# Layer 2's gate and value products by one level of Strassen, and the exponentials divided in place on GpSimd

## The chip, the core and the metric

The kernel runs on one core of one Trainium2 chip. Its engines work side by side, each through its own queue in order: TensorE (PE in the rows; PEld is its weight load), VectorE (DVE), ScalarE (ACT), GpSimd (POOL), and SyncE (SP), which issues the DMAs. The metric is the device time of one execution in microseconds.

## The reference

```python
# attention: batch 2, 12 heads, 448 positions, head dimension 64
scores = (1 / np.sqrt(64)) * np.matmul(q, k.transpose(0, 1, 3, 2))
scores = np.where(mask, -1e9, scores)              # causal
attn = np.exp(scores - np.max(scores, axis=-1, keepdims=True))
attn = attn / (np.sum(attn, axis=-1, keepdims=True) + 1e-09)
x = np.matmul(attn, v)                             # then 896 tokens x 768
# layer 1: d_ff 2048
h = x @ w_in
g = (a[0] + a[1] * h + a[2] * h**2 + a[3] * h**3) / (1 + abs(b[0]) * abs(h) + abs(b[1]) * h**2 + 1e-6)
x = g @ w_out
# layer 2: d_ff 1536
gate = 1.0 / (1.0 + np.exp(-(x @ w_gate)))
val = x @ w_val
return (gate * val) @ w_out
```

The weights come as float64 and are turned into float32 on the chip.

## The kernel before

Every product of the two layers is made of three matmuls: both operands are split into a high part (fp32r) and a low part (what is left), and high x high, high x low and low x high are summed in PSUM. So a weight costs, after its DMA on SP (`raw`, 768 KB), two ScalarE passes and one VectorE pass that make float32 (`val`), a copy to the high part and a subtraction on GpSimd for the low part (`weight`, L145 to L176). An activation costs a copy (ScalarE) and a subtraction (GpSimd).

**Attention** runs over 12 pairs of heads, each in three groups of query tiles, (0, 1), (2), (3), of 112 queries each; a tile t has (t+1) x 112 keys. For a group: `scores` on TensorE (L442), `maximum` on VectorE with the mask (L450), `exponentials` on ScalarE with the row sum (L464), `turn`, which transposes the exponentials on TensorE (L482), `copied` out of PSUM (L490, L492), and at the end of the pair `values`, the product with v (L519). The exponentials are not divided. In their place `inverses` (L470, L471) makes the reciprocals of the sums, once a pair; `factors` (L501) spreads them over the 64 rows of a head by small matmuls against the identity; `factors_out` (L511) copies them out on ScalarE; `result` (L528) multiplies the values by them on VectorE; `result_hi` (L535) and `result_lo` (L540, GpSimd but for the last pair of a batch) split the result into `xh` and `xl`.

**Layer 1** goes in 4 chunks of 512 features and two parts of the tokens (0 to 447 and 448 to 895 in chunk 0, 0 to 383 and 384 to 895 afterwards): `in1_tile` gives h, `rational` g (six VectorE operations a tile, L275 to L285), `out1_tile` sums into `y1` and, in the last chunk, splits y1 into xh and xl again (L331, L334).

**Layer 2** goes in 6 chunks of 256 features and the two parts of the tokens: `gate_tile` and `val_tile` (both through `up`, L252 to L258), 6 steps along d_model for each block of 128 features, then the sigmoid, the product and its split (L355 to L361); `out2_tile` (L365) sums 14 output tiles of 128 x 384 into `y2` (L389), one chunk at a time, and the last chunk writes them out (L392). The first gate tile is woven between the last output tiles of layer 1 (`woven("1110111", ...)`).

**The order.** All work is listed as jobs with an engine, an estimated cost, what they wait for and a rank. `in_turn` (L36) plays them through: on each engine the ready job with the lowest rank goes next. The order found is fixed as the order of each queue. TensorE's order of the two layers' products is a chain (`unit`); attention's steps run two groups ahead (`LA = 2`), with two PSUM tiles for scores and transposes in turn, and the products of layer 1's chunk 0 fill gaps among them. Weights come in `portion`s through two raw and two val buffers in turn.

## Time and profile before

| | |
|---|---|
| median of three timed runs | 603.45 us |
| the three runs | 603.12, 603.45, 603.87 us |
| span of the profiled execution, first to last instruction | 601.4 us |
| TensorE busy | 593.5 us (99%) |
| VectorE, ScalarE, GpSimd busy | 358.0, 357.2, 254.4 us |
| attention with the first products of layer 1 | 0 to about 124 us |
| layer 1 | to about 344 us |
| layer 2 | to 598 us, the last write to 601.4 us |

A busy share is an average; which engine ends a stretch is read from the chain of waits and from the stretches one by one. Matmuls are pipelined, so a matmul's own duration in a row is longer than its share of TensorE's time; the distance between two starts is that share.

### The profile page before, as it was taken

What the parts mean: (1) busy time and instruction counts of PE and PEld (TensorE: products, weight loads), DVE (VectorE), ACT (ScalarE), POOL (GpSimd) and SP (SyncE); (2) the same over time, 40 slices, a digit from 0 to 9 for tenths busy, and PEclk for the clock granted to TensorE, in tenths of its full rate; (3) what the DMA queues carried; (4) which work ended last, traced back from release to release, by engine and by line L of the source; (5) the groups of instructions that cost most, each with busy time, mean ns of one, the idle gap of its engine ahead of it and who ended that gap; (6) DMA issues with size and microseconds to landing.
All of it is one profiled execution on the core that took longest, in us unless ns stands there. A gap on an engine that the chain in (4) does not pass through costs nothing.

```text
span 601.4 us, 8821 instructions
## 1 busy us (share of the span) xinstructions
PE 593.5 (99%) x3352; PEld 511.6 (85%) x3352; DVE 358.0 (60%) x677; ACT 357.2 (59%) x686; POOL 254.4 (42%) x193
## 2 busy tenths in 40 slices
PE   7999999999999999999999999999999999999997
PEld 5566666689988998898898989989989989989987
DVE  5877899938968986789685243246336335312314
ACT  6888888858897793859396448766344444111010
POOL 0634321357529656534746465545145144211010
PEclk9999999999999999999999999999999999999999
DMA  7645340045413351323421054645324123000004
GB/s 242 207 173 158 118 166 16 6 157 166 146 53 110 108 195 53 113 88 123 152 59 51 2 158 158 210 157 161 102 105 159 54 105 106 0 1 1 0 14 170
DMA packets 25641, 65.05 MB, mean 108 GB/s; under 512 B 1984, under 2 KB 3776, under 8 KB 25600
## 3 DMA queue, kind: packets, MB, share of 16 engines
q1 hardware_dynamic: 25600, 64.50, 32.7%
q8 instruction: 26, 0.43, 0.3%
q14 instruction: 15, 0.12, 0.1%
HBM read 61.74 MB, written 2.75 MB: 107 GB/s over the span
## 4 chain that ended last, share of the span: by engine, by line
PE 97%; DVE 2%; issue 0%; ACT 0%; DVEq 0%
PE h L256 7%; PE o L314 6%; PE h L258 6%; PE h L257 6%; PE o L315 6%; PE o L316 6%; PE z L381 5%; PE z L379 5%; PE z L380 5%; PE gu L257 5%; PE gu L258 5%; PE gu L256 5%; PE vu L257 5%; PE vu L256 5%; PE vu L258 5%; PE s L442 4%
## 5 line engine op out<-in xcount | busy, mean ns | idle before, releaser
L361 POOL TENSOR_TENSOR gl<-pr_u,gh 128x384 fp32r<-128x384 f32 (+1 forms) x24 | 27.7, 1153 | 111.5 <-ACT gh L359 111.5
L289 POOL TENSOR_TENSOR gl_h<-t_h,gh_h 128x384 fp32r<-128x384 f32 (+2 forms) x32 | 39.2, 1226 | 84.0 <-ACT gh_h L287 83.9
L256 PE MATMUL h<-xh,wh_in 128*128 128x384 f32 (+2 forms) x192 | 71.3, 371 | 0.0
L314 PE MATMUL o<-gh_h,oh_out 128*128 128x384 f32 (+2 forms) x192 | 70.3, 366 | 0.0
L315 PE MATMUL o<-gl_h,oh_out 128*128 128x384 f32 (+2 forms) x192 | 69.9, 364 | 0.0
L316 PE MATMUL o<-gh_h,ol_out 128*128 128x384 f32 (+2 forms) x192 | 69.9, 364 | 0.0
L258 PE MATMUL h<-xh,wl_in 128*128 128x384 f32 (+2 forms) x192 | 69.7, 363 | 0.0
L257 PE MATMUL h<-xl,wh_in 128*128 128x384 f32 (+2 forms) x192 | 69.7, 363 | 0.0
L176 POOL TENSOR_TENSOR ol_out<-val_out,oh_out 128x768 fp32r<-128x768 f32 x28 | 55.1, 1971 | 26.7 <-ACT oh_out L174 25.4
L389 DVE TENSOR_TENSOR y<-y,z 128x384 f32<-128x384 f32 x70 | 38.3, 552 | 32.2 <-PE z L381 32.1
L357 DVE TENSOR_TENSOR pr_u<-sg_u,vu 128x384 f32<-128x384 f32 (+1 forms) x24 | 14.8, 617 | 70.8 <-PE vu L258 68.4
L381 PE MATMUL z<-oh_out,gl 128*128 128x384 f32 x168 | 56.2, 335 | 0.0
L379 PE MATMUL z<-oh_out,gh 128*128 128x384 f32 x168 | 56.2, 335 | 0.0
L380 PE MATMUL z<-ol_out,gh 128*128 128x384 f32 x168 | 56.2, 334 | 0.0
L164 DVE SCALAR_TENSOR_TENSOR val_out<-raw_out 128x768 uint32<-128x768 uint32 x28 | 35.7, 1277 | 31.3 <-ACT raw_out L161 23.4
L464 ACT ACTIVATE e<-e,sc 112x112 f32<-112x112 f32 (+3 forms) x96 | 49.7, 522 | 6.5 <-DVE sc L450 6.3
L258 PE MATMUL gu<-xh,wl_gate 128*128 128x384 f32 (+1 forms) x144 | 52.2, 363 | 0.0
L257 PE MATMUL gu<-xl,wh_gate 128*128 128x384 f32 (+1 forms) x144 | 52.2, 363 | 0.0
L257 PE MATMUL vu<-xl,wh_val 128*128 128x384 f32 (+1 forms) x144 | 52.1, 362 | 0.0
L256 PE MATMUL gu<-xh,wh_gate 128*128 128x384 f32 (+1 forms) x144 | 52.1, 362 | 0.0
L256 PE MATMUL vu<-xh,wh_val 128*128 128x384 f32 (+1 forms) x144 | 52.1, 362 | 0.0
L258 PE MATMUL vu<-xh,wl_val 128*128 128x384 f32 (+1 forms) x144 | 52.1, 362 | 0.0
(89 smaller groups left out, 1425.5 us busy)
## 6 DMA issues: line engine op xcount, KB each, us to landing
raw_out<-in_moe_w_out_dram SPq DMA_DIRECT2D x28, 768.0 KB, 4.3
raw_in<-in_moe_w_in_dram SPq DMA_DIRECT2D x16, 768.0 KB, 4.5
raw_gate<-in_moe_w_gate_dram SPq DMA_DIRECT2D x12, 768.0 KB, 4.3
raw_val<-in_moe_w_val_dram SPq DMA_DIRECT2D x12, 768.0 KB, 4.3
qk<-in_qk_dram SPq DMA_DIRECT2D x12, 448.0 KB, 5.7
v<-in_v_dram SPq DMA_DIRECT2D x12, 224.0 KB, 3.8
out_dram<-y SPq DMA_DIRECT2D x14, 192.0 KB, 1.8
a_sb<-in_moe_a_dram SPq DMA_DIRECT2D x1, 2.0 KB, 7.1
```

The costliest lines, as they stand in the source:

```text
L176: nc.gpsimd.tensor_tensor(lo, vf, hi, op=ALU.subtract)
L256: nc.tensor.matmul(ps, hi[:, c, fs], xh[:, c, bs], start=(c == 0), stop=False)
L257: nc.tensor.matmul(ps, hi[:, c, fs], xl[:, c, bs], start=False, stop=False)
L258: nc.tensor.matmul(ps, lo[:, c, fs], xh[:, c, bs], start=False, stop=(c == KC - 1))
L289: nc.gpsimd.tensor_tensor(gl, t, gh, op=ALU.subtract)
L314: nc.tensor.matmul(ps, hi[:, es], gh, start=(i == 0), stop=False)
L315: nc.tensor.matmul(ps, hi[:, es], gl, start=False, stop=False)
L316: nc.tensor.matmul(ps, lo[:, es], gh, start=False, stop=(i == NF - 1))
L379: nc.tensor.matmul(ps, gh[:, ms], hi[:, ns], start=(i == 0), stop=False)
L380: nc.tensor.matmul(ps, gh[:, ms], lo[:, ns], start=False, stop=False)
L381: nc.tensor.matmul(ps, gl[:, ms], hi[:, ns], start=False, stop=(i == NF2 - 1))
L464: nc.scalar.activation(e, e, AF.Exp, bias=d["sc"][:, t, j : j + 1], scale=-1.0, accum_out=d["sum"][:, t, j : j + 1])
```

## The change

**Strassen in layer 2.** For one unit (a block of 128 features, of gate and value together) the two weights are the rows of a 2 x 2 matrix of blocks, gate and value by the lower and upper half of d_model; the activations are the columns, lower and upper half of d_model by the first and second 448 tokens. Winograd's form makes the four results from seven block products in place of eight. Sums of weights (`weight_sums`, four a unit) and of activations (`act_sum`, once) are made in float32 first and then split into high and low. Each block product is 3 steps of 3 matmuls of 448 columns. Four PSUM banks A to D hold the products of a unit; `combine` adds them up, some in PSUM itself. Weights and activations lie in two large rooms cut up by hand, ten slots for weights. There are 12 units; the output products go over groups of two units, but the last two groups have one unit each. The order at the seam is: all of layer 1's output tiles, then units 0 (in an order of its own), 1 and 2, then output groups and units in turn.

**Division in place.** `inverses` runs for each group, `normalised` multiplies the exponentials by the reciprocals on GpSimd before they are transposed, and `factors`, `factors_out` and `result` go. The values in PSUM are split straight away, `result_lo` on VectorE always. The values get a second PSUM tile.

The planner's ranks and costs are set anew, and it takes in a cost for a change of TensorE's tiling mode. The diff, cut to its core:

```diff
+    PRODUCTS = {
+        "p1": ("a11", "b11", "A", True),
+        "p6": ("s2", "t2", "B", True),
+        "p7": ("s3", "t3", "C", True),
+        "p5": ("s1", "t1", "D", True),
+        "p2": ("a12", "b21", "A", False),
+        "p4": ("a22", "t4", "C", False),
+        "p3": ("s4", "b22", "D", False),
+    }
...
+    def weight_sums(u, k):
+        a = {n: halves[u, n] for n in ("a11", "a12", "a21", "a22", "s1", "s2", "s3", "s4")}
+        if k == 0:
+            nc.vector.tensor_tensor(a["s1"], a["a21"], a["a22"], op=ALU.add)
+            nc.vector.tensor_tensor(a["s2"], a["s1"], a["a11"], op=ALU.subtract)
+        else:
+            nc.vector.tensor_tensor(a["s3"], a["a11"], a["a21"], op=ALU.subtract)
+            nc.vector.tensor_tensor(a["s4"], a["a12"], a["s2"], op=ALU.subtract)
...
+    def weight_hi(u, name):
+        nc.scalar.copy(slot(u, name)[0], halves[u, PRODUCTS[name][0]])
+    def weight_lo(u, name):
+        hi, lo = slot(u, name)
+        nc.gpsimd.tensor_tensor(lo, halves[u, PRODUCTS[name][0]], hi, op=ALU.subtract)
...
+    def act_lo(name, c):
+        eng = nc.vector if name in BY_VECTOR else nc.gpsimd
+        eng.tensor_tensor(act[name][1][:, c], act_from(name, c), act[name][0][:, c], op=ALU.subtract)
+    def product(u, name, c):
...
+        nc.tensor.matmul(ps, hi[:, c], bh[:, c], start=begins, stop=False, skip_group_check=True)
+        nc.tensor.matmul(ps, hi[:, c], bl[:, c], start=False, stop=False, skip_group_check=True)
+        nc.tensor.matmul(ps, lo[:, c], bh[:, c], start=False, stop=ends, skip_group_check=True)
+    def combine(u, what):
...
+        if what == "p1":
+            nc.scalar.copy(x, ps["A"])
+        elif what == "u2":
+            nc.vector.tensor_tensor(x, x, ps["B"], op=ALU.add)
+        elif what == "u3":
+            nc.vector.tensor_tensor(y, x, ps["C"], op=ALU.add)
+        elif what == "c22":
+            nc.vector.tensor_tensor(y, y, ps["D"], op=ALU.add)
+        elif what == "sg1":
+            nc.scalar.activation(z, ps["A"], AF.Sigmoid)
+        elif what == "c21":
+            nc.vector.tensor_tensor(ps["C"], x, ps["C"], op=ALU.add)
+        elif what == "pr1":
+            nc.vector.tensor_tensor(z, z, ps["C"], op=ALU.mult)
+        elif what == "c12":
+            nc.vector.tensor_tensor(ps["D"], x, ps["D"], op=ALU.add)
+        elif what == "sg2":
+            nc.scalar.activation(ps["D"], ps["D"], AF.Sigmoid)
+        elif what == "pr2":
+            nc.vector.tensor_tensor(y, y, ps["D"], op=ALU.mult)
...
-    def inverses(n):
-        rs = T[n]["sum"]
+    def inverses(n, k):
+        rs = T[n]["sum"][:, GROUPS[k][0] : GROUPS[k][-1] + 1]
         nc.vector.tensor_scalar_add(rs, rs, 1e-9)
         nc.vector.reciprocal(rs, rs)
+    def normalised(n, t, j):
+        e = T[n]["e", t, j]
+        nc.gpsimd.tensor_scalar(e, e, T[n]["sum"][:, t, j : j + 1], 1.0, op0=ALU.mult, op1=ALU.mult)
...
     def result_hi(n):
-        nc.scalar.copy(xh[x_part(n)], T[n]["xn"])
+        nc.scalar.copy(xh[x_part(n)], T[n]["x"])
     def result_lo(n):
-        eng = nc.vector if pairs[n][1] == NP - 1 else nc.gpsimd
-        eng.tensor_tensor(xl[x_part(n)], T[n]["xn"], xh[x_part(n)], op=ALU.subtract)
+        nc.vector.tensor_tensor(xl[x_part(n)], T[n]["x"], xh[x_part(n)], op=ALU.subtract)
...
-            [("exp", n, t, j) for t in GROUPS[k] for j in both] + freed_by("s"),
-            rank + R_TURN,
+            [("norm", n, t, j) for t in GROUPS[k] for j in both] + freed_by("s"),
+            rank + R["turn"],
...
+    GROUPS2 = [(u, u + 1) for u in range(0, NU - 2, 2)] + [(NU - 2,), (NU - 1,)]
...
-    woven("1110111", stage_in2(0, 0), stage_out(*ins[-1]))
+    _run(stage_out(*ins[-1]))
+    sums_of_x()
+    unit_of_weights(0, ("p1", "p5", "p2", "p7", "p6", "p4", "p3"))
+    unit_of_weights(1, PRODUCTS)
+    unit_of_weights(2, PRODUCTS)
```

## Rows read from the trace of the kernel before

**Rows 1.** The page: TensorE's busy time, granted clock and DMA rate by slice.

```profile
PE 593.5 (99%) x3352; PEld 511.6 (85%) x3352; DVE 358.0 (60%) x677; ACT 357.2 (59%) x686; POOL 254.4 (42%) x193
...
PEclk9999999999999999999999999999999999999999
...
GB/s 242 207 173 158 118 166 16 6 157 166 146 53 110 108 195 53 113 88 123 152 59 51 2 158 158 210 157 161 102 105 159 54 105 106 0 1 1 0 14 170
```

**Rows 2.** The page, the chain that ended last: shares of the span by engine.

```profile
PE 97%; DVE 2%; issue 0%; ACT 0%; DVEq 0%
```

**Rows 3.** Stretches: length, busy time of PE, PEld, DVE, ACT, POOL; clock; DMA.

```profile
0.00:124.00 124.00, 119.63 (x928) 76.04 (x929) 98.72 (x302) 100.89 (x274) 39.96 (x39) 1.00 0.42 138
80.00:100.00 20.00, 20.00 (x148) 13.67 (x146) 17.79 (x50) 16.32 (x45) 4.93 (x4) 1.00 0.17 51
120.00:140.00 20.00, 20.00 (x104) 17.17 (x103) 8.55 (x9) 11.55 (x18) 11.80 (x8) 1.00 0.49 157
345.00:601.40 256.40, 252.89 (x1324) 235.50 (x1322) 97.04 (x123) 98.71 (x146) 87.05 (x57) 1.00 0.30 97
```

**Rows 4.** TensorE in order of time: start, duration, line, first matmuls of a stage.

```profile
134.06 0.37 PE L256 MATMUL h<-xh,wh_in 128*128 128x448 f32 x1
...
148.94 0.34 PE L256 MATMUL h<-xh,wh_in 128*128 128x384 f32 x1
...
161.43 0.36 PE L314 MATMUL o<-gh_h,oh_out 128*128 128x448 f32 x1
...
523.35 0.39 PE L256 MATMUL gu<-xh,wh_gate 128*128 128x512 f32 x1
...
539.71 0.33 PE L379 MATMUL z<-oh_out,gh 128*128 128x384 f32 x1
```

**Rows 5.** The chain in order of time: start, time on the chain, what.

```profile
5.60 0.28 DVE e L450
...
21.30 0.92 PE r L501 x16
...
121.45 2.04 PE x L519 x16
```

**Rows 6.** VectorE's groups, 0 to 124 us: count, busy us, mean ns, idle before.

```profile
L528 DVE TENSOR_TENSOR xn<-xn,x 128x448 f32<-128x448 f32 x12 | 7.4, 614 | 2.2 <-PE x L519 1.9 <-ACT xn L511 0.3
...
L470 DVE TENSOR_SCALAR sum<-sum 112x8 f32<-112x8 f32 x12 | 3.6, 300 | 0.0
...
L284 DVE SCALAR_TENSOR_TENSOR d_h<-z_h,one,d_h 128x448 f32<-128x448 f32 x4 | 2.7, 685 | 0.1
...
L471 DVE RECIPROCAL sum<-sum 112x8 f32<-112x8 f32 x12 | 2.4, 203 | 0.4
```

**Rows 7.** VectorE and GpSimd in order of time around 64.5 us.

```profile
64.45 1.83 POOL L176 TENSOR_TENSOR ol_out<-val_out,oh_out 128x768 fp32r<-128x768 f32 x1
...
64.54 1.77 DVE L470 TENSOR_SCALAR sum<-sum 112x8 f32<-112x8 f32 x1
```

**Rows 8.** GpSimd's groups over the span, shapes apart.

```profile
L176 POOL TENSOR_TENSOR wl_val<-val_val,wh_val 128x768 fp32r<-128x768 f32 x12 | 23.5, 1958 | 15.6 <-ACT wh_val L174 13.7 <-PE z L381 1.8
...
L361 POOL TENSOR_TENSOR gl<-pr_u,gh 128x512 fp32r<-128x512 f32 x12 | 15.5, 1291 | 53.9 <-ACT gh L359 53.9
...
L172 POOL TENSOR_SCALAR oh_out<-val_out 128x768 fp32r<-128x768 f32 x16 | 13.4, 836 | 16.2 <-DVE val_out L164 15.1 <-PE o L315 1.0
...
L361 POOL TENSOR_TENSOR gl<-pr_u,gh 128x384 fp32r<-128x384 f32 x12 | 12.2, 1015 | 57.6 <-ACT gh L359 57.6
...
L334 POOL TENSOR_TENSOR xl<-y,xh 128x448 fp32r<-128x448 f32 x6 | 7.6, 1272 | 1.6 <-ACT xh L331 1.6
```

**Rows 9.** One first group, in order of time: its last row sum, its transposes.

```profile
48.40 0.20 ACT L464 ACTIVATION_READ_ACCUMULATOR e<-e,sc 112x1 f32 x1
...
51.12 0.79 PE L482 MATMUL p<-ident,e 112*112 112x112 f32 x6
```

**Rows 10.** VectorE's timeline: four output sums in a row.

```profile
320.63 1.94 DVE L326 TENSOR_TENSOR y<-y,o 128x384 f32<-128x384 f32 x4
```

More of the change, by code (lines that the diff above doesn't have):

```diff
@@ L365, in out2_tile @@
-    def out2_tile(c, m, n):
-        half = m // 4
+    PRODUCTS = {
[7 more added lines that the diff above has]
+    }
+    first, second = slice(0, S), slice(S, NT)
+    lows, highs = slice(0, KH), slice(KH, KC)
+    act = {"b11": (xh[:, lows, first], xl[:, lows, first]), "b21": (xh[:, highs, first], xl[:, highs, first])}
@@ new lines, in combine @@
+    def combine(u, what):
+        ps = {b: unit_ps.get((u, b)) for b in "ABCD"}
+        if what in ("p1", "u3", "sg1"):
+            n = {"p1": "x", "u3": "y", "sg1": "z"}[what]
+            unit_sb[u, n] = tmp.tile([P, 512], F32, tag="t1" if n == "y" else "t0", name=f"{n}_{u}")[:, :S]
+        x, y, z = (unit_sb.get((u, n)) for n in "xyz")
+        gh, gl = store["g"][u % NG2]
+        if what == "p1":
[18 more added lines that the diff above has]
+            nc.vector.tensor_tensor(y, y, ps["D"], op=ALU.mult)
+        else:
+            t, ns = (z, first) if what[-1] == "1" else (y, second)
+            if what[:2] == "gh":
+                nc.scalar.copy(gh[:, ns], t)
+            else:
+                nc.gpsimd.tensor_tensor(gl[:, ns], t, gh[:, ns], op=ALU.subtract)
@@ L368, in out2_tile @@
+    def out2_tile(group, m_, n):
+        us = GROUPS2[group]
+        half = m_ // 4
         if half not in y2:
@@ L692, in tile_causal_attention__moe_rational__moe_glu, with weights_out2 @@
+    def weights_out2(u):
+        key = ("out2", u, 0)
+        free = [("out", NCH - 1, 1, KC - 1, "mm", NF - 1)]
+        if u >= 4:
+            group = next(k for k, us in enumerate(GROUPS2) if u - 4 in us)
+            free = [("out2", group, ready[B] - 1, 1, "mm", len(GROUPS2[group]) - 1)]
+        group = next(k for k, us in enumerate(GROUPS2) if u in us)
+        portion((*key, 0), rows(wt, key, w_out2, u), free, ("out2", group, 0, 0, "mm", GROUPS2[group].index(u)))
     tiles = {}
     unit = None
-    n_tiles = [0, 0]
+    n_tiles = [0, 0, 0]
@@ L712, in place @@
         n_tiles[after] += 1
-        ring = "b" if after and n_tiles[1] % 6 > 1 else "a"
-        deps = freed_by(ring, 4 if ring == "b" else 2) + ["late"] * after
-        freed[ring].append([(*key, "after", read)])
+        if key[:3] == ("out", NCH - 1, 1) or key[0] == "out2":
+            n_tiles[2] += 1
+            r = "ad"[n_tiles[2] // 2 % 2]
+        else:
+            r = "b" if after and n_tiles[1] % 6 > 1 else "a"
+        deps = freed_by(r, 4 if r == "b" else 2) + ["late"] * after
+        freed[r].append([(*key, "after", read)])
+        ring[key] = r
         return deps
@@ L764, in stage_out @@
                 matmuls(key, i, deps + [("out", c, i, 0, 5), ("in", c, b, i, "after", 5)], UNIT[width(c, b)], out1_tile)
-            follow(key, scaled(stages, c, b, 0.15 * (c > 0) * b), at["end"] + R_SUM)
+            follow(key, scaled(stages, c, b, 0.15 * (c > 0) * b), at["end"] + R["sum"])
             yield
-    def stage_in2(c, b):
-        for i in range(NF2):
-            kg, kv = ("gate", c, b, i), ("val", c, b, i)
-            for key, make in ((kg, gate_tile), (kv, val_tile)):
-                deps = place(kv, 0 if key == kg else 1)
-                for u in range(KC):
-                    w = [(key[0], c, 0, u // 3, 5), ("out", NCH - 1, b, u, "after", 2)]
-                    matmuls(key, u, deps + w, UNIT[width(1, b)], make)
-            followed(kv, scaled(GLU, 1, b), ("out2", c, ready[b], 0, "mm", i), [("in", NCH - 1, 1, NF - 1, "after", 2)])
-            yield
@@ new lines, in stage_out2 @@
+    def stage_out2(group):
+        stages = [("ACT", 0.48) if group == 0 else ("DVE", 0.55)]
+        if group == len(GROUPS2) - 1:
+            stages.append(("SP", 0.1))
+        sums = [("out", NCH - 1, k, KC - 1, "after", 2) for k in range(B)] + [("tl", "t4", KH - 1)]
+        for b in range(B):
+            for m in range(ready[b], ready[b + 1]):
+                for n in range(2):
+                    key = ("out2", group, m, n)
+                    deps = place(key, 0) + (sums if group == 0 else [])
+                    for i, u in enumerate(GROUPS2[group]):
+                        gs = [("e", u, f"gl{k + 1}") for k in range(b + 1)]
+                        matmuls(key, i, deps + [("out2", u, 0, 0, 5), *gs], UNIT2, out2_tile)
+                    follow(key, stages, at["end"] + R["sum"])
+                    yield
```

405 lines of the change are left out of this document (258 added, 147 removed).

## The prediction, made before the change was built

> **What bounds the kernel now.** I read the page's first two parts before anything else: TensorE is busy 99% of the span, and its granted clock is full in every slice, which is the 2.4 GHz level [rows 1]. A busy share of matmuls can flatter, so I then read the chain of waits: it runs through TensorE for 97% of the span and through VectorE for 2% [rows 2]. So products taken away shorten the kernel, as long as no other engine comes to stand in their place. Whether one does is asked of two stretches, in the table of stretches [rows 3]: attention (the first 124 us, where the weights and the first chunk of layer 1 are woven in) has VectorE at 98.7 of 124 us and ScalarE at 100.9, both close behind TensorE; layer 2 (from 345 us on) has VectorE at 97, ScalarE at 99 and GpSimd at 87 of 256 us. Layer 2 has room, attention has little. Between them (124 to 316 us) the change does nothing but rename buffers. The sum is made on the profiled execution's span, 601.4 us; the median of the timed runs, 603.45, lies 2.0 us above it, and these 2.0 us are added at the end.
>
> **Layer 2's gate and value products.** Before: 12 blocks of 128 features, for gate and value, over 6 chunks of the contraction, 3 products each, for 384 and for 512 tokens: 864 matmuls. From start to start in the trace, 72 of 512 columns take 539.71 - 523.35 = 16.36 us (0.2272 each), 72 of 384 take 161.43 - 148.94 = 12.49 us in layer 1 (0.1735 each) [rows 4]. One chunk is both, 28.85 us, and there are 6: 173.1 us. After: 12 units x 7 products x 3 chunks of the contraction x 3 = 756 matmuls, all of 448 columns. Layer 1 has that shape: 72 of 448 take 148.94 - 134.06 = 14.88 us, 0.2067 each [rows 4]. So 756 x 0.2067 = 156.2 us and the gain is 16.9 us, not the eighth (21.6) that the count of products promises: 448 columns cost 3.3% more per column than the mean of 384 and 512. The output products keep count and shape.
>
> By the Trainium skill ("TensorE: Matmul & The Clock Gate", section Back-to-back issue gap) the isolated gap between warm matmuls is the columns over 2.4 GHz plus 2.5 ns; by that 448 columns would step at 189 ns and the two old shapes at 163 and 216, and the gain would be 20.4 us. The rows disagree, each step is longer and 448 is off the line through the other two, so the rows' figure stands.
>
> **What that moves to the other engines** is, per unit: seven weight highs and lows of 128x384 in place of two pairs of 128x768, four sums of weights, and ten PSUM operations in place of four. A 128x384 low took 1.02 us on GpSimd [rows 8], an operation of VectorE with a PSUM operand of 448 columns 0.61 [rows 6]. GpSimd gains 7 x 1.02 - 2 x 1.96 = 3.2 us a unit, 39 in all: 126 of some 240 us. VectorE gains four sums of 0.55 to 0.61 and five operations of 0.61, some 5.4 us a unit, and 14 output sums more: some 170 of 240. ScalarE gains about 2.5 a unit, some 130. All fit beside 13.0 us of products a unit plus 7.3 of output products, so I cost them at nothing; if that cover fails it is a rival below.
>
> **The seams.** (1) In unit 0 the order is p1, p5, p2, p7, p6, p4. p4 adds into the bank of p7, which must first be read by u3, which waits for u2, which waits for p6, the product directly ahead of p4: two operations of 0.61 and two handoffs of about 0.2 stand bare, 1.6 us. In later units two products (3.7 us) lie between, which covers it. (2) Before, gate products were woven into the last output stage of layer 1; now nothing is. GpSimd has, for each of the last three of that stage's tiles, lows of 64 and 448 columns and two lows of sums (three of 448 at 1.27 [rows 8] and, in proportion, 0.2 to 0.3 for the small one: 4.1 us), while TensorE gives a tile every 12 x 0.227 = 2.7 us. So it is 4.2 us behind at the end and has a last 4.1 to do, 8.3; p1, p5, p2 and p7 give four times 1.86, 7.4. That is a little short, and the lows of unit 1's weights queue behind it: 1.5 us, between 0 and 5. (3) The last two output groups have one unit each, so a tile comes every 0.52 us and no longer every 1.04. VectorE did four sums of 128x384 in a row in 1.94 us, a step of 0.46 [rows 10], so it keeps up; 14 writes of 192 KB now leave within 7.3 us, 377 GB/s, against 242 GB/s at most in a slice of the page [rows 1]. 0.7 us, between 0 and 4.
>
> **Attention.** Removed from TensorE: the 16 small matmuls that spread the reciprocals, 0.92 us from start to start, 12 times [rows 5]: 11.0 us. ScalarE loses one copy a pair (0.5). Now the other side. VectorE loses the multiplication (12 x 0.61) and gets the residue of x from GpSimd (11 x 0.61, in the shape of that multiplication), and in place of one pair of small operations per head pair (about 0.17 + 0.20; the 0.30 mean holds one stall) it has three: 24 x 0.37 = 8.9 us more [rows 6]. 98.7 - 7.4 + 6.7 + 8.9 - 1.6 (that stall [rows 7]) = 105.3 us. It starts at 5.6 us; the last value product ended at 123.5 [rows 5], less 11.0 is 112.5. So 105.3 us of VectorE stand in 106.9: in 80 to 100 us, where it was fullest, it reached 89% [rows 3]. What can slip out behind attention is the rational of the last two tiles of chunk 0 (twice six operations, the one in [rows 6] at 0.69, some 8.2 us) and a weight or two. If all of it slips, the gain stays 11; if none does, VectorE at 95% ends attention at 116.4, at 89% at 123.9, which gives back 4 to 11.
>
> The divisions go to GpSimd and into the chain from exponentials to transposes. No row has that shape there: 128x768 with two constants took 0.84 [rows 8], which bounds 448 columns by 0.49 (in proportion) and 0.84 (no cheaper); with the fixed part that the subtractions show (1.02 at 384, 1.29 at 512 [rows 8]) I take 0.57, 0.47, 0.38 and 0.28 for the four widths, 3.4 us a pair, 41 in all. GpSimd goes from 40.0 [rows 3], less ten residues of x at 1.27, to 68 us: room enough. But the first group's chain grows by 0.37 + 4 divisions (1.3) + handoffs (0.4), 2.1 us, where the sums were ready at 48.60 and the transposes began at 51.12 [rows 9]: 2.5 us of slack, which shrinks with the shorter period. Any 1.8 us subtraction ahead of the divisions on GpSimd then holds TensorE. Together I take 6 us given back of the 11.0, between 1 and 12: nearer the middle since VectorE needs over 90% of the stretch or must let work slip, and the slack is used up but not overdrawn.
>
> One row speaks against small VectorE operations beside a busy GpSimd: a 112x8 scalar operation that usually takes 0.17 took 1.77 us and ended as GpSimd's subtraction did, 64.45 + 1.83 = 66.28 against 66.31 [rows 7]. The Trainium skill ("GPSIMD Engine Reference", section Key points) says that GpSimd shares its SBUF interfaces with VectorE and contends with it in two-port modes or with two SBUF inputs; the trace agrees in that one place. After, there are 36 such operations, not 12. If GpSimd spends 19 of some 113 us on subtractions there (eight weight lows of 1.96, four of gl) and 41 on divisions of 0.4, one of them meets a wait of 0.9 or 0.2 us in the mean of these, some 0.2 us, 8 us in all; without such waits nothing. That lies inside the two ends taken above.
>
> **The sum.** 601.4 - 11.0 - 16.9 + 6.0 + 1.6 + 1.5 + 0.7 = 583.3, with 2.0 around the span 585.3 us. Its own range: 580 (giveback 1, seams as taken) to 593 (giveback 11, seams 6).
>
> **Rivals.**
> - *The reciprocals' gain holds in full.* The slipped work fits behind attention, which has VectorE at 8.6 of 20 us from 120 on [rows 3], and the seams close: giveback 1, seams 2, so 601.4 - 27.9 + 3 + 2 = 578.5. Against it: the 89%. Chance 0.17.
> - *VectorE becomes attention's bound.* Nothing slips, the small operations stall behind GpSimd: giveback 11 to 12 in place of 6, 591. For it: [rows 6, 7]. Chance 0.18.
> - *Layer 2 starves.* The weights of a unit come late (raw buffers are held until the last weight sum's low is made), 1.4 us a unit eats the 16.9: 602. Against it: half the time of GpSimd free. Chance 0.08; a third of it lies within 0.2%.
> - *Slower: the divisions stand bare in attention's loop.* If GpSimd's long subtractions run ahead of the first group's divisions, TensorE stands 2.1 us or more a pair for that group and some for the others. From 2.0 us a pair on (24 us, what is left of 27.9 after the seams) nothing is gained; 2.5 us a pair gives 609. Against it: 2.5 us of slack, and GpSimd idle nearly half of the stretch. Chance 0.07.
>
> **Chances.** Forecast 0.50, and the four above. Faster by over 0.2% (what a measurement here can tell from no change): 0.50 + 0.17 + 0.18 + 0.05 = 0.90; within it 0.03; slower 0.07. The range leaves out the two last rivals and the low edge of the first: 578 to 594.
>
> **What would show it.** Matmuls of 448 columns in layer 2 that step at 0.207 (wrong if 0.20 or below); attention's last value product at 115 to 120 us with VectorE over 90% busy; TensorE idle there before transposes, put down to GpSimd's divisions (first group above all) or before scores, put down to VectorE; a gap of some 1.6 us ahead of unit 0's p4; no gaps between units. The forecast is wrong if attention ends below 113 or above 122, or if TensorE waits in every unit of layer 2.

## The result, and the profile after

The changed kernel takes 597.0 us (median of four runs, 596.2 to 597.67) against 603.66 us for the kernel before beside it: a ratio of 0.989, 95% interval [0.9876, 0.9904]. It is faster, by 6.6 us (1.1%) and not by the 18 us forecast, and the time lies 3 us above the range. The profiled execution has a span of 594.4 us against 601.4.

The page of the kernel after: busy time of the engines, TensorE's granted clock in 40 slices, and the chain's shares by engine. These answer to [rows 1, 2].

```profile
PE 574.9 (97%) x3052; PEld 490.3 (82%) x3052; DVE 448.0 (75%) x860; ACT 381.8 (64%) x755; POOL 359.3 (60%) x345
...
PEclk8898999899999999999999999999999999999999
...
PE 83%; DVE 9%; POOL 3%; ACT 2%; issue 2%; POOLq 0%; DVEq 0%; ACTq 0%
```

TensorE's busy time is 18.6 us less, but it is no longer busy without a break: the chain runs through VectorE for 9% and through GpSimd for 3% of the span, where it was 2% and none [rows 2]. And the clock is not full in every slice: four of the first eight are down. Both signs lie in the first 124 us, which the stretches of the kernel after show (columns as in [rows 3], first the four that answer to those rows):

```profile
0.00:124.00 124.00, 110.79 (x681) 65.39 (x682) 105.75 (x336) 93.06 (x254) 77.75 (x119) 0.94 0.40 132
80.00:100.00 20.00, 19.88 (x126) 13.66 (x124) 19.40 (x57) 18.28 (x48) 10.66 (x15) 1.00 0.22 70
120.00:140.00 20.00, 20.00 (x122) 14.74 (x121) 11.54 (x27) 11.97 (x29) 9.07 (x14) 1.00 0.23 79
345.00:594.40 249.40, 243.06 (x1256) 227.88 (x1255) 165.62 (x250) 134.40 (x231) 147.75 (x120) 1.00 0.32 107
```

TensorE was busy 119.6 of the first 124 us before and is 110.8 now. VectorE reaches 19.40 of 20 us at 80 to 100, where it had 17.79. Layer 2 is clean: full clock, and TensorE busy for 97% of it though VectorE has 69 us more to do there and GpSimd 61 us more.

**Where the 7.0 us of the span come from.** Layer 1's last output product ended at 343.38 us in the kernel before, and 6.27 us of layer 2's gate and value products were woven in ahead of it, so layer 1 alone would have ended at 337.1. Now layer 2's first product starts at 344.02 (row below). Layer 2 took 601.4 - 337.1 = 264.3 us and takes 594.4 - 344.0 = 250.4: 13.9 us won, where 13.1 were forecast. All before it got 6.9 us longer, where 5 us less were forecast. The whole miss is there.

TensorE of the kernel after in order of time (start, duration): two block products of unit 0, and a later stretch of two units:

```profile
344.02 0.36 PE L458 MATMUL u_A<-xh,room_a 128*128 128x448 f32 x1
...
345.85 0.36 PE L458 MATMUL u_D<-xh,room_a 128*128 128x448 f32 x1
...
440.81 0.36 PE L458 MATMUL u_A<-xh,room_a 128*128 128x448 f32 x1
...
466.85 0.34 PE L512 MATMUL z<-oh_out,room_b 128*128 128x384 f32 x1
```

From 440.81 to 466.85 lie 2 x 63 matmuls of 448 columns: 26.04 us, 0.2067 each, the step of [rows 4] to the last digit. In unit 0 it is 1.83 us for 9, 0.2033, and units 1 and 2 run at 0.2026.

In attention the new work is read from three views. The groups of VectorE in the first 140 us (count, busy us, mean ns, idle before) that answer to [rows 6]:

```profile
L602 DVE TENSOR_SCALAR sum<-sum 112x2 f32<-112x2 f32 x24 | 9.6, 402 | 1.7 <-ACT e L596 1.5
...
L652 DVE TENSOR_TENSOR xl<-x,xh 128x448 fp32r<-128x448 f32 x12 | 7.5, 621 | 8.3 <-ACT xh L649 8.3
...
L603 DVE RECIPROCAL sum<-sum 112x2 f32<-112x2 f32 x24 | 4.0, 166 | 0.8
L602 DVE TENSOR_SCALAR sum<-sum 112x4 f32<-112x4 f32 x12 | 3.0, 251 | 0.2 <-ACT e L596 0.2
L603 DVE RECIPROCAL sum<-sum 112x4 f32<-112x4 f32 x12 | 2.1, 178 | 0.4
```

The reciprocals cost what they should. The additions (L602) have means of 402 and 251 ns, but their median is 166: a few are very long. And the groups of GpSimd there, shapes apart, which have no row before:

```profile
L607 POOL TENSOR_SCALAR e<-e,sum 112x448 f32<-112x448 f32 x24 | 15.8, 673 | 13.7 <-DVE sum L603 10.2 <-ACT pt L626 2.7 <-ACT xh L649 0.4
L607 POOL TENSOR_SCALAR e<-e,sum 112x224 f32<-112x224 f32 x24 | 15.0, 637 | 0.0
L607 POOL TENSOR_SCALAR e<-e,sum 112x336 f32<-112x336 f32 x24 | 14.4, 611 | 3.8 <-DVE sum L603 2.5 <-PE p L618 0.4 <-PE h L262 0.4
L607 POOL TENSOR_SCALAR e<-e,sum 112x112 f32<-112x112 f32 x24 | 9.7, 417 | 25.3 <-DVE sum L603 12.8 <-ACT e L596 7.9 <-ACT d_h L285 2.8
```

The divisions take 417, 637, 611 and 673 ns for one to four tiles of keys, 54.9 us in all. I had taken 0.28, 0.38, 0.47 and 0.57. That 224 columns take longer than 336 says that something else than their length is in it, and the order of time shows what. One first group of the kernel after, with VectorE beside it, which answers to [rows 9]:

```profile
109.53 0.17 DVE L602 TENSOR_SCALAR sum<-sum 112x4 f32<-112x4 f32 x1
109.73 0.18 DVE L603 RECIPROCAL sum<-sum 112x4 f32<-112x4 f32 x1
...
110.11 3.64 POOL L607 TENSOR_SCALAR e<-e,sum 112x112 f32<-112x112 f32 x4 [2.63 <-DVE sum L603]
...
110.23 1.08 DVE L628 COPY pt<-p 112x896 f32<-112x896 f32 x1
...
111.24 0.67 DVE L287 SCALAR_TENSOR_TENSOR t_h<-t_h,a_sb,d_h 128x448 f32<-128x448 f32 x1
...
111.94 0.69 DVE L288 SCALAR_TENSOR_TENSOR d_h<-z_h,one,d_h 128x448 f32<-128x448 f32 x1
...
112.19 0.31 PE L618 MATMUL p<-ident,e 112*112 112x112 f32 x1 [0.45 <-POOL e L607]
...
112.67 0.76 DVE L289 SCALAR_TENSOR_TENSOR t_h<-d_h,t_h 128x448 f32<-128x448 f32 x1
...
113.80 0.40 PE L618 MATMUL p<-ident,e 112*112 112x112 f32 x2 [0.39 <-POOL e L607]
114.13 0.30 PEld L636 LDWEIGHTS x<-pt,v 112*64 112x64 f32 x4
114.13 3.26 PE L636 MATMUL x<-pt,v 112*64 112x448 f32 x10
```

The sums of this group had been ready since 108.7 but VectorE came to them at 109.53. Then four divisions took 3.64 us while VectorE copied and ran three passes of the rational (L287 to L289), and the transposes waited for the divisions one after another. In another first group (55.73 in the next fence) the same four take 1.55 us, though VectorE makes the same copy beside them (55.45). So it is not the copy that tells the two groups apart but what VectorE does behind it: the passes of the rational in the slow group, an addition that is itself held up in the quick one. That these passes cause the delay is read from two groups and was not tested by itself. A hold in the other direction is plainer. VectorE and GpSimd of the kernel after around 50 to 59 us, which answers to [rows 7]:

```profile
50.35 3.50 DVE L172 SCALAR_TENSOR_TENSOR val_out<-raw_out 128x768 uint32<-128x768 uint32 x1
...
55.45 1.06 DVE L628 COPY pt<-p 112x896 f32<-112x896 f32 x1
...
55.73 1.55 POOL L607 TENSOR_SCALAR e<-e,sum 112x112 f32<-112x112 f32 x4 [0.94 <-DVE sum L603]
...
56.43 2.65 DVE L602 TENSOR_SCALAR sum<-sum 112x2 f32<-112x2 f32 x1
...
57.24 1.81 POOL L184 TENSOR_TENSOR ol_out<-val_out,oh_out 128x768 fp32r<-128x768 f32 x1
```

The addition ends at 59.08, GpSimd's subtraction at 59.05. A pass of 128x768 on VectorE that takes 0.95 us at the least (0.96 and 1.05 in the medians of its two kinds in attention) took 3.50 while GpSimd went through two divisions and a subtraction, which ended at 53.04.

In both places TensorE is short of work, and right after it its clock is down. Stretches of the kernel after, the first 20 us and four of 4 us:

```profile
0.00:20.00 20.00, 15.84 (x78) 9.77 (x78) 10.69 (x49) 11.46 (x34) 7.85 (x23) 0.83 0.58 182
52.00:56.00 4.00, 2.29 (x14) 1.59 (x14) 3.96 (x9) 2.27 (x11) 2.15 (x3) 1.00 0.83 289
56.00:60.00 4.00, 4.00 (x16) 1.39 (x14) 3.96 (x6) 1.76 (x4) 3.58 (x7) 0.57 0.64 262
108.00:112.00 4.00, 2.15 (x13) 1.05 (x13) 3.90 (x11) 2.98 (x10) 1.90 (x2) 1.00 0.00 0
112.00:116.00 4.00, 2.92 (x11) 1.28 (x13) 3.59 (x10) 1.33 (x3) 3.85 (x6) 0.76 0.01 2
```

TensorE is busy 2.29 and 2.15 of 4 us, and in the next stretch the granted clock is 0.57 and 0.76 in the mean: part of it at the 1.2 GHz level. A third fall lies at the very start, 0.83 over the first 20 us, where the kernel before has 1.00 with TensorE busy for 16.69 us; it makes up 3.4 us, about half of all that the clock loses. Not every wait ends so: at 60 to 80 us TensorE is idle for 1.4 us and the clock stays at 1.00. The value products at 114.13 took 3.69 us on the chain where the same ones take 2.04 at the end, at 133.33:

```profile
114.20 3.69 PE x L636 x16
133.33 2.04 PE x L636 x16
```

The last value product ends at 135.4 us; before it was 123.5 [rows 5]. By then twice as many of layer 1's output steps are woven in (15 against 7 or 8, some 5 us), so about 7 of these 11.9 us are a loss.

### The profile page after: what moved, and what is told of

Its sections match the earlier page's. It is cut to its first block, busy times and chain, and to the rows that moved or that the text cites. A ratio compares the mean times of both kernels' runs of the same rounds, so it can differ in the third digit from the quotient of the medians.

```text
span 594.4 us, 8892 instructions
## 1 busy us (share of the span) xinstructions
PE 574.9 (97%) x3052; PEld 490.3 (82%) x3052; DVE 448.0 (75%) x860; ACT 381.8 (64%) x755; POOL 359.3 (60%) x345
## 4 chain that ended last, share of the span: by engine, by line
PE 83%; DVE 9%; POOL 3%; ACT 2%; issue 2%; POOLq 0%; DVEq 0%; ACTq 0%
PE o L319 6%; PE o L321 6%; PE o L320 6%; PE h L260 6%; PE h L261 6%; PE h L262 6%; PE z L512 5%; PE z L514 5%; PE z L513 5%; PE x L636 3%; PE p L618 2%; PE u_D L458 2%; PE u_D L459 2%; PE u_D L460 2%; PE u_C L459 2%; PE u_C L460 2%
## 5 line engine op out<-in xcount | busy, mean ns | idle before, releaser
L607 POOL TENSOR_SCALAR e<-e,sum 112x112 f32<-112x112 f32 (+3 forms) x96 | 54.5, 585 | 42.7 <-DVE sum L603 25.5
L423 POOL TENSOR_TENSOR room_a<-val,room_a 128x384 fp32r<-128x384 f32 x30 | 35.1, 1180 | 42.3 <-ACT room_a L419 34.7
L512 PE MATMUL z<-oh_out,room_b 128*128 128x384 f32 x168 | 56.1, 334 | 0.0
L514 PE MATMUL z<-oh_out,room_b 128*128 128x384 f32 x168 | 56.1, 334 | 0.0
L513 PE MATMUL z<-ol_out,room_b 128*128 128x384 f32 x168 | 56.1, 334 | 0.0
L423 POOL TENSOR_TENSOR room_a<-raw,room_a 128x384 fp32r<-128x384 f32 x38 | 45.2, 1207 | 10.9 <-ACT room_a L419 6.1
L582 DVE CUSTOM_DVE_ANT_0 e<-s,mask 112x112 f32<-112x112 f32 (+3 forms) x96 | 38.4, 444 | 9.2 <-PE s L574 8.0
L618 PEld LDWEIGHTS p<-ident,e 112*112 112x112 f32 x240 | 24.8, 139 | 24.7 <-POOL e L607 13.6
L321 PE MATMUL o<-room_b,ol_out 128*128 128x512 f32 (+1 forms) x96 | 36.9, 384 | 0.0
L320 PE MATMUL o<-room_b,oh_out 128*128 128x512 f32 (+1 forms) x96 | 36.9, 384 | 0.0
L319 PE MATMUL o<-room_b,oh_out 128*128 128x512 f32 (+1 forms) x96 | 36.8, 384 | 0.0
L261 PE MATMUL h<-xl,room_a 128*128 128x448 f32 (+2 forms) x96 | 35.0, 364 | 1.7 <-DVE xl L652 1.7
L260 PE MATMUL h<-xh,room_a 128*128 128x448 f32 (+2 forms) x96 | 36.3, 378 | 0.0
L262 PE MATMUL h<-xh,room_a 128*128 128x448 f32 (+2 forms) x96 | 34.9, 364 | 0.0
```

Of the source, the lines that this page charges most:

```text
L260: nc.tensor.matmul(ps, hi[:, c, fs], xh[:, c, bs], start=(c == 0), stop=False)
L261: nc.tensor.matmul(ps, hi[:, c, fs], xl[:, c, bs], start=False, stop=False)
L262: nc.tensor.matmul(ps, lo[:, c, fs], xh[:, c, bs], start=False, stop=(c == KC - 1))
L319: nc.tensor.matmul(ps, hi[:, es], gh, start=(i == 0), stop=False)
L320: nc.tensor.matmul(ps, hi[:, es], gl, start=False, stop=False)
L321: nc.tensor.matmul(ps, lo[:, es], gh, start=False, stop=(i == NF - 1))
```

## The experiments

For most runs three numbers tell what happened in attention: TensorE's busy time in the first 140 us, its granted clock there, and the start of layer 2's first product, u_A. Against the kernel before (135.63 busy, clock 1.00, 337.1 for the end of layer 1), idle time and lost clock add up as below (the clock is given in hundredths, so its column is good to about 0.7 us); "sum" is -11.0 (the factor products that are gone) + more idle + lost clock, and "measured" is the start of u_A less 337.1.

| kernel | time, us | idle | (1 - clock) x 140 | sum | measured |
|---|---|---|---|---|---|
| before | 603.5 | 4.4 | 0 | | 0 |
| after | 597.0 | 13.2 | 7.0 | +4.8 | +6.9 |
| e3, short divisions | 590.8 | 10.9 | 5.6 | +1.1 | +0.5 |
| e4, nobody waits for the divisions | 589.6 | 12.0 | 2.8 | -0.6 | +0.9 |
| e5, no additions | 592.0 | 10.4 | 7.0 | +2.1 | +2.1 |
| e11, e4 and e5 together | 585.0 | 8.8 | 1.4 | -5.2 | -4.0 |
| e7, true costs | 594.7 | 15.0 | 2.8 | +2.5 | +5.8 |
| e12, true costs, no additions | 591.1 | 11.1 | 2.8 | -1.4 | +1.0 |
| e9, Strassen alone | 591.4 | 5.7 | 0 | +1.3 (nothing removed) | +2.1 |

The sum follows the measured shift from run to run, within 2.1 us in six rows, but falls short of it by 3.3 us in e7 and by 2.4 in e12. So idle time and clock are most of the loss and not all of it; what the rest is the runs do not show. Nor does the sum name a cause: that is for the experiments. The stretch 0 to 140 us of the kernels before, after, e5 and e11, one fence each (columns as in [rows 3]):

```profile
0.00:140.00 140.00, 135.63 (x1005) 90.59 (x1006) 105.67 (x308) 110.45 (x289) 51.76 (x47) 1.00 0.42 139
```

```profile
0.00:140.00 140.00, 126.79 (x777) 77.05 (x778) 113.32 (x350) 101.74 (x270) 85.42 (x129) 0.95 0.38 128
```

```profile
0.00:140.00 140.00, 129.57 (x801) 81.56 (x802) 103.51 (x315) 101.84 (x272) 90.33 (x131) 0.95 0.40 133
```

```profile
0.00:140.00 140.00, 131.19 (x831) 85.80 (x832) 104.94 (x321) 108.48 (x282) 101.88 (x137) 0.99 0.46 150
```

**One part at a time.** e1 keeps the attention of the kernel before and takes layer 2 from the changed one.

```diff
-    def inverses(n, k):
-        rs = T[n]["sum"][:, GROUPS[k][0] : GROUPS[k][-1] + 1]
+    def inverses(n):
+        rs = T[n]["sum"]
...
-    def normalised(n, t, j):
...
+    def factors(n):
...
+    def factors_out(n):
...
+    def result(n):
+        nc.vector.tensor_tensor(T[n]["xn"], T[n]["xn"], T[n]["x"], op=ALU.mult)
```

> Attention as before (undivided exponentials, factors spread by matmuls, the planner's ranks and costs of before for it), layer 2 by Strassen as in the changed kernel. If the two parts add up and attention alone made the loss, layer 2 keeps the 14.1 us that the two traces show for it: 603.7 - 14.1 = 589 to 590 us, attention's last value product at 123 to 124 us, TensorE's clock full. Rival: the new rooms, buffers or planner rules slow attention too, then about 597 and attention's end well behind 124 us.

Measured: 597.64 us, 0.9896 [0.9872, 0.992]: the rival's time, but not for its reason. Attention was as before and layer 2 began at 337.8, but took 258.1 us. The miss was mine: I had taken the estimated costs and ranks of the kernel before along, so the order in layer 2 was not the changed kernel's. e6 corrected the costs but not the rank of the sums of layer 1's last output stage, e9 that too, which makes layer 2's order that of the changed kernel on every engine.

```diff
-            follow(key, scaled(stages, c, b, 0.15 * (c > 0) * b), at["end"] + R_SUM)
+            follow(key, scaled(stages, c, b, 0.15 * (c > 0) * b), at["end"] + (R["sum"] if c else R_SUM))
```

> As the first run (attention of before, layer 2 by Strassen), but the planner's costs and handoffs of before are kept for attention alone, and the layers get those of the changed kernel. In the first run layer 1 ended 5.6 us earlier than in the changed kernel, and layer 2 took 7 us longer with TensorE idle between its units. If that loss came from the planner's older costs, it goes: 589 to 591 us, with layer 2's stretch as in the changed kernel (250 us from its first product). If layer 2 loses it whenever attention ends early (its weights come too late), 596 to 598 us.

> Strassen's products with the attention of the kernel before (factor products, no divisions), and now the order of layer 1's last output stage and of layer 2 exactly that of the changed kernel on all engines. Theory (layer 2 gained its 13 to 14 us, and what the changed kernel lacks was lost in attention): last value product starts at 121 to 123 us, layer 2 starts at 337.6 to 339 and lasts 250 to 251, span 588 to 590, time 590 to 592. Rival (the late start of layer 2 seen in the two earlier attempts belongs to the Strassen part itself): layer 2 lasts 255 or more, time 595 to 597.

Measured: e6 595.63 us, 0.9879 [0.9855, 0.9903]; e9 591.43 us, 0.9799 [0.9785, 0.9814]. In e6 TensorE waited in unit 0 for the copies of xh and lows of xl that the late sums had pushed back, and the clock was 0.91 at 340 to 360 us. e9's time is the one that its theory gave. Those waits are gone in it and layer 2 lasts 590.0 - 339.2 = 250.8 us:

```profile
L458 PE MATMUL u_A<-xh,room_a x60: 362/368/475, 339.2 to 567.0; 128*128 128x448 f32 x60
```

So Strassen's layer 2 is worth its 13 us without the division part (12.1 us of the whole time), and this kernel beats the changed one by 5.6 us. One rank of a sum ahead of the seam was worth 4.2 us.

e2 does the other part alone: its edit is made on the kernel before, whose layer 2 stays, and the planner gets the ranks and costs of the changed kernel.

```diff
-    def inverses(n):
-        rs = T[n]["sum"]
+    def inverses(n, k):
+        rs = T[n]["sum"][:, GROUPS[k][0] : GROUPS[k][-1] + 1]
...
+    def normalised(n, t, j):
+        e = T[n]["e", t, j]
+        nc.gpsimd.tensor_scalar(e, e, T[n]["sum"][:, t, j : j + 1], 1.0, op0=ALU.mult, op1=ALU.mult)
...
-    def factors(n):
...
-    def result(n):
-        nc.vector.tensor_tensor(T[n]["xn"], T[n]["xn"], T[n]["x"], op=ALU.mult)
```

> Attention as in the changed kernel (division on GpSimd, its ranks and costs), layer 2 as before. If the division alone makes the loss, attention ends near 135 us with 15 output steps woven in and the whole is 603.7 + 6.9 = 610 to 611 us, slower than before. Rival: the loss needs the Strassen part beside it (weights that come earlier, rooms), then 598 to 604 us.

Measured: 611.06 us, 1.0133 [1.0116, 1.015], as expected for a loss that the division part makes alone. By itself the division part makes the kernel 7.6 us slower. It saves 11.0 us of matmuls and gives back 18 to 19.

**Is TensorE still what the loop costs?** e8 puts 12 small matmuls of 64 columns into each pair, ahead of the value products. They were meant to take about as much of TensorE as the factors did.

```diff
-            d["x"] = ps_x.tile([P, 512], F32, tag="x", name=f"x_{n}")[:, :S]
+            room = ps_x.tile([P, 512], F32, tag="x", name=f"x_{n}")
+            for i in range(12):
+                nc.tensor.matmul(room[:D, S:], ident[:CP, :D], ident[:CP, : 512 - S], start=True, stop=True)
+            d["x"] = room[:, :S]
```

> The changed kernel with 12 small matmuls put in ahead of each pair's value products (into 64 spare columns of its bank, waiting for nothing of their own): TensorE gets back about as much as the factors took, some 0.8 to 1 us a pair, 10 to 12 us in all, with the order unchanged. If TensorE is not what bounds attention any more, most of it hides: 597 to 600 us. If it still is: 606 to 609 us.

Measured: 608.62 us, 1.0088 [1.0071, 1.0105]: 11.6 us more than the changed kernel. The last value product starts at 145.16, 11.8 later. The time fell into the range of 606 to 609, but by luck, since more was put in than meant. The chain of e8 at its last pair:

```profile
143.68 1.48 PE x L636 x23
145.16 1.95 PE x L639 x16
```

The 12 matmuls of the program stand in the trace as 24, as the 8 factor products of a pair stand there as 16, and they take 1.48 us, where those 16 took 0.92 [rows 5]. Over twelve pairs that is some 17 us, of which 11.6 came out at the end. So most of TensorE's time in this loop still counts, but about a third of what was added does not come out, in a loop in which TensorE has 13 us of idle time. The loop goes round TensorE, VectorE, ScalarE and GpSimd, and of the three engines that were tried none passes its time on in full: the runs that follow get 6.2 us for 24.8 of GpSimd (e3) and 5.0 us for 12.6 of VectorE (e5). ScalarE was not tried.

**What in the division part costs.** e3 shortens the divisions to eight columns each and leaves their place, their count and all waits as they are (the rest of the exponentials stays undivided).

```diff
-        nc.gpsimd.tensor_scalar(e, e, T[n]["sum"][:, t, j : j + 1], 1.0, op0=ALU.mult, op1=ALU.mult)
+        nc.gpsimd.tensor_scalar(e[:, :8], e[:, :8], T[n]["sum"][:, t, j : j + 1], 1.0, op0=ALU.mult, op1=ALU.mult)
```

> The changed kernel with the division made for 8 columns of each tile of exponentials alone (the rest stays undivided): same instructions, same waits, same order, GpSimd's time in attention down by some 25 to 30 us. If the length of the divisions (on GpSimd, in the chain from exponentials to transposes, and in front of VectorE's operations that wait for GpSimd) makes the loss, most of TensorE's 13.6 us of waits for them go: 587 to 590 us. If VectorE's own added instructions are the bound, they are all still there: 594 to 596 us.

Measured: 590.76 us, 0.9786 [0.9771, 0.9801], just above the first range. 24.8 us less of GpSimd's time gave 6.2 us. But most of the waits that were to go are still there: those of TensorE's weight loads for divisions fell from 13.6 to 10.1 us only. The group itself is the surprise:

```profile
L607 POOL TENSOR_SCALAR e<-e,sum 112x8 f32<-112x8 f32 x96 | 30.1, 336 | 54.9 <-DVE sum L603 36.9 <-ACT e L596 9.7 <-ACT d_h L285 3.4
```

Eight columns still take 336 ns (273 in the median), where 112 columns take 361 at the least in the changed kernel: most of a short division does not go with its length.

e4 writes the divided values to tiles that nothing reads, so that the transposes wait for the exponentials alone (the result is then not normalised).

```diff
-        nc.gpsimd.tensor_scalar(e, e, T[n]["sum"][:, t, j : j + 1], 1.0, op0=ALU.mult, op1=ALU.mult)
+        e2 = e2p.tile([CP, (t + 1) * CP], F32, tag=f"f{t}", name=f"f_{n}_{t}_{j}")
+        nc.gpsimd.tensor_scalar(e2, e, T[n]["sum"][:, t, j : j + 1], 1.0, op0=ALU.mult, op1=ALU.mult)
...
-            [("norm", n, t, j) for t in GROUPS[k] for j in both] + freed_by("s"),
+            [("exp", n, t, j) for t in GROUPS[k] for j in both] + freed_by("s"),
```

> The changed kernel with the divided exponentials written to tiles of their own that nobody reads, and the transposes made from the undivided ones, waiting for the exponentials alone: GpSimd and VectorE do all they did, but neither reciprocal nor division stands in the chain (the result is not divided). If the chain's length makes the loss: 585 to 589 us. If it is the load, VectorE's or the contention between GpSimd and VectorE, little goes: 594 to 597 us.

Measured: 589.62 us, 0.977 [0.9756, 0.9785]. All the work is there, only nobody waits for the divisions: 7.4 us less, just above the range for the chain's length and far from that for the load. The clock loss falls from 7.0 to 2.8 us, the idle time by 1.2.

e5 drops the addition of 1e-9 to the sums, 36 small VectorE operations (the sums are far larger, so this leaves only that guard out).

```diff
-        nc.vector.tensor_scalar_add(rs, rs, 1e-9)
         nc.vector.reciprocal(rs, rs)
```

> The changed kernel without the addition of 1e-9 to the row sums (each sum is at least 1, so it changes nothing), the same order otherwise: 36 operations of VectorE go, 12.6 us of its time with the waits behind GpSimd that it spends in them, and 0.17 us or more of each group's chain. If VectorE is attention's bound beside the chain: 588 to 591 us. If the chain through GpSimd alone decides, only some 36 x 0.17 at most: 594 to 596 us.

Measured: 592.02 us, 0.9811 [0.9796, 0.9825]: 5.0 us less, between the two ranges and nearer the one in which VectorE is a bound beside the chain. The 36 additions had been busy for 12.6 us (9.6 + 3.0, fence above); at their median of 166 ns they would have taken 6.0, and the rest is holds behind GpSimd.

e11 joins e4 and e5.

> The changed kernel with its divided exponentials written to tiles that nothing reads (so the result is not normalised, and the transposes wait for the exponentials alone), and without the additions of 1e-9. If the wait for the divisions and VectorE's added work are two separate costs, their gains of 7.4 and 5.0 us add: 584 to 585, last value product starts near 118. If the additions cost only as a link of the chain from exponentials to transposes, nothing is gained over 589.6: 589 to 590.

Measured: 585.0 us, 0.9693 [0.9678, 0.9707], and the last value product starts at 118.2. 597.0 - 7.4 - 5.0 = 584.6: they add. So the wait for the divisions and VectorE's load are two costs, and the additions did not cost as a link of the division chain, since here no transpose hangs on it. Together they are 12.0 us. Layer 2 begins at 333.1:

```profile
L458 PE MATMUL u_A<-xh,room_a x60: 362/368/469, 333.1 to 560.4; 128*128 128x448 f32 x60
```

e10 asks whether an addition costs in the attention of the kernel before as well; it is e9 without its 12.

> As the run before, without the one addition of 1e-9 to the sums that each pair has there (12 in all; the sums are far larger). If a small operation of VectorE costs attention time wherever it stands (the 24 to 36 additions gave 5 us in the changed kernel): 12 of 0.17 to 0.40 us, 2 to 4 us less than the run before. If it costs only where the divisions wait behind it: no difference, within 0.5 us.

Measured: 591.19 us, 0.9796 [0.9781, 0.981], 0.24 us below e9, which is no difference. TensorE stands still nowhere between 20 and 100 us in e9 (20.00 of 20 in each of the four stretches), so there a microsecond of VectorE is hidden. My two alternatives had been wherever it stands, and only where the divisions wait behind it; e10 and e11 together refute both. What remains is that it costs where the loop has no TensorE work left to cover it; that is argued from the idle time, not tested by itself.

**Mends.** e7 gives the planner division times near the measured ones, 0.40 to 0.66 us in place of 0.20 to 0.57, which changes only the order.

```diff
-    NORM = (0.2, 0.32, 0.45, 0.57)
+    NORM = (0.40, 0.56, 0.60, 0.66)
...
-        job(("inv", n, k), "DVE", 0.31, [("exp", n, t, j) for t in GROUPS[k] for j in both], rank + R["inv"], inverses, n, k)
+        job(("inv", n, k), "DVE", 0.45, [("exp", n, t, j) for t in GROUPS[k] for j in both], rank + R["inv"], inverses, n, k)
```

> The changed kernel with the planner's costs of the divisions (0.20, 0.32, 0.45, 0.57 us) put at 0.40, 0.56, 0.60 and 0.66 and of the two small operations on the sums at 0.45 in place of 0.31, near what the trace shows: the instructions are the same, their order is found anew. If much of the loss is an order made for divisions that are too short: 590 to 593 us. If the loss lies in the work itself, within 1.5 us of the changed kernel's 597.

> The changed kernel ordered with division times as measured (0.40 to 0.66 us, not 0.20 to 0.57) and without the additions of 1e-9: the two mends that keep its result. If they add (2.3 and 5.0 us): 589 to 590. If both only shift the same idle time: 591 to 593. Below the run with Strassen alone only if the divisions are worth having at all: 588 or less.

Measured: e7 594.73 us, 0.9856 [0.9841, 0.987], 2.3 us less, which lies between its two ranges and decides for neither. e12, the same without the additions, 591.08 us, 0.9798 [0.9773, 0.9824], falls to its second range. Of 2.3 + 5.0 they kept 5.9; that is 0.9 below e5, less than the spread of e12's own four runs (589.42 to 592.63), so beside the missing additions the new order shows no gain. So the mended division part and no division part at all come to the same time, 591.1 and 591.4: with both mends it gives back just what it saves.

## Why the prediction was wrong

- **Layer 2 was right.** Products: forecast 0.2067 a step, gain 16.9 us. Measured: units 1 and 2 at 0.2026, unit 0 at 0.2033 between its waits, the rest at 0.2067; 189 x 0.203 + 567 x 0.2067 = 155.6 us against 173.1, a gain of 17.5. I had said that a step of 0.20 would prove me wrong; it comes near that for three units, and why these run faster stays open. It is not the instructions: in e4, e5, e6 and e9 units 1 and 2 step at 0.2067 too. (By these steps 448 columns cost 3.2% more per column than the mean of the other two widths, not 3.3%.) By the Trainium skill's rule ("TensorE: Matmul & The Clock Gate", section Back-to-back issue gap), named in the prediction, a step would be 0.189; no unit of the trace has that.
- **The seams were right in sum.** Forecast 1.6 + 1.5 us. Unit 0 goes from 344.02 to 360.09, 16.07 us, where 63 steps of 0.2033 make 12.8: 3.3 us. The waits of TensorE in layer 2 (total, count, longest) are these three, all in unit 0:

```profile
PE u_C L458 <- DVE y L475: 1.5, 1, 1.5
PE u_C L459 <- POOL room_b L447: 0.5, 1, 0.5
PE u_A L458 <- ACT x L471: 0.3, 1, 0.3
```

  The first is the bank of p7 which u3 (L475) has to read, ahead of p4: 1.5 for my 1.6. The second is the end of GpSimd's lows, of which I gave 1.5 in all. No wait in any later unit, so the rival in which layer 2 starves is out. The matmuls behind these three gaps also run long (0.44, 0.47 and 0.47 in place of 0.36).
- **The tail was right.** 0.7 forecast; from the start of the last matmul to the end it is 4.4 us (590.02 to 594.4) against 3.9 (597.55 to 601.4), 0.5 more. The output sums kept up, at a step of 0.50 (which answers to [rows 10]):

```profile
578.91 12.03 DVE L522 TENSOR_TENSOR y<-y,z 128x384 f32<-128x384 f32 x24
```

- **The 11.0 us of factor products were right as time of TensorE.** They are gone from the trace. That they were worth 11.0 us of the whole is not shown: in e8 some 17 us of TensorE put in cost 11.6.
- **The step that failed is the giveback in attention:** 6.0 us, with 1 and 12 as its ends; it measured 17.9 (11.0 + 6.9), with the 11.0 counted in full. The last value product ended at 135.4, or some 130 without the steps of layer 1 that moved ahead of it, so beyond the 122 at which I had said that the forecast would be wrong. What the runs put in its place is the wait of the transposes for the divisions, 7.4 us (e4), and VectorE's additions, 5.0 us (e5), which add (e11: 12.0). Three pieces of the giveback were wrong:
  1. *The divisions.* I took 0.28 to 0.57 us from the shape of the subtractions, 41 us in all; they took 0.42 to 0.67, 54.9 us. The fixed part was set too low: eight columns take 0.34 (e3). And four divisions beside VectorE's passes took more than double the time of four others (3.64 us against 1.55).
  2. *The slack of the first group.* I set 2.5 us of slack against 2.1 of chain and called it used up but not overdrawn. A quick first group does take 2.1 us, from the addition at 55.16 to the last division at 57.28, but a disturbed one takes 4.2 (109.53 to 113.75). The view of waits puts 13.6 us of waits of TensorE's weight loads on the divisions, in 27 waits of at most 1.3. Half a microsecond often, not 2 us per pair. The second row is the other sign that I had named, scores held by VectorE:

```profile
PEld p L618 <- POOL e L607: 13.6, 27, 1.3
PEld s L574 <- DVE sc L582: 8.9, 14, 1.7
```

  3. *The clock.* I did not have it in the sum at all: the granted clock was 1.00 everywhere in [rows 1, 3], and I never asked what it would do once TensorE waits. It fell three times, once in the first 20 us and twice behind gaps, and cost up to 7.0 us, beside 8.8 us of more idle time. Of the 17.9 us, 15.8 are accounted for by these two; 2.1 are not.
- **VectorE's load was near as a number, and wrong as a cost.** I forecast 105.3 us for it, and the first 124 us hold 105.75. But attention is not done by then, so the two are not the same work and the agreement is in part luck: the additions and reciprocals alone took 18.7 us (9.6 + 4.0 + 3.0 + 2.1) against 6.0 before [rows 6], 12.7 more, where the sum had 7.3 more (8.9 - 1.6). VectorE reaches 18 to 19 of 20 us in four stretches (80 to 100 us is shown above), the share that I had doubted, and pays for it by holding scores and sums back. The stalls of the additions behind GpSimd came true: 12.6 us where 36 of the median 166 ns would be 6.0, so 6.6 of the 8 us that I had for them. I then counted them as lying inside the two ends; the additions were a term of their own, since e5's gain adds to e4's.
- **Two rivals share the truth.** One was that VectorE becomes attention's bound (chance 0.18, a giveback of 11 to 12 us), the other that the divisions stand bare in attention's loop (chance 0.07, 2.0 us a pair and more). Attention gave back 1.5 us a pair (17.9 / 12), between the two, and e4, e5 and e11 show a part of each at once. I had them as alternatives, and I left the second its small chance because GpSimd was idle for half of the stretch. Idle in the mean is no answer to a chain: GpSimd is idle because it waits for VectorE's reciprocals (25.5 us of such waits), and TensorE then waits for GpSimd.
- **The forecast's 585.3 us is what e11 measures** (585.0): the changed kernel if no transpose waits for the divisions and VectorE is spared the additions. Its giveback is 11.0 - 4.0 = 7.0 us, near the forecast's 6.0. That is luck and no confirmation: the forecast had counted the additions and the longer chain in, and e11 has neither.

What stays open: the 2.1 us; the 7.0 us that e11 still gives back, in which GpSimd's divisions, the residue of x that moved to VectorE (7.5 us there, L652) and the new ranks stand together, none of them timed alone; and how much of the loss VectorE and GpSimd cause by slowing each other rather than by their own length. That VectorE is held up by GpSimd is read from the rows at 50.35 and 56.43, and that divisions run slowly beside VectorE's passes from those at 110.11; no run takes the contention away and leaves the rest.

## What to carry to other kernels

When a step moves to an idle engine and into a chain that runs round several engines, cost it by the chain, disturbed durations included, and not by the idle share of the engine. Where TensorE's clock has been full in a kernel in which TensorE hardly waits, ask what the clock will do once it waits, and put that into the price: here 7.0 us came on top of 8.8 us of idle time. And when two changes come in one diff, forecast and time them one by one: here one was worth 12 us and the other took 6 of them back.

## What the hardware showed that I had not expected

- A GpSimd scalar operation on 112x8 float32 elements takes 273 ns in the median, 336 in the mean; on 112x112 at least 361.
- VectorE was held up by GpSimd: an addition on 112x2 elements, 166 ns in the median of its line, took 2.65 us and ended with GpSimd's subtraction, and a pass of 0.95 us took 3.50. The other direction is likely and less plain: four GpSimd divisions took 3.64 us beside passes of the rational, and 1.55 us elsewhere. The Trainium skill ("GPSIMD Engine Reference", section Key points) says that GpSimd shares its SBUF interfaces with VectorE and contends with it in 2-port modes or with two SBUF inputs. The rows agree that the two hold each other up; they do not show which operands it takes. In this loop the 36 additions on two or four columns, holds included, cost 5.0 us (e5).
- TensorE's granted clock was 0.57 in the mean over the 4 us behind a stretch in which it was busy 2.29 of 4 us, and 0.76 behind one with 2.15.
- The same matmul of 448 columns steps at 0.2026 us in units 1 and 2 and at 0.2067 from then on, with no wait in either; in e9, with the same order in layer 2, it steps at 0.2067 in all of them.
